# Keeping the state of a chunked scan for two heads' columns instead of four, and reading it in 32x64 tiles

## The chip, the cores and the metric

The kernel runs on one core of a Trainium2 chip. The metric is the device time of one execution in microseconds, as a median over several executions. Beside the timed runs, one execution was recorded by the hardware profiler. In its output PE is TensorE (matmuls), PEld its weight loads, DVE is VectorE, ACT is ScalarE, POOL is GpSimd and SP is SyncE, which here issues nearly all DMAs.

## What is computed

Two blocks follow each other. The first is a state-space scan in chunks (Mamba 2), for 4 batches, 8 heads, 768 positions, head dimension D = 32 and state dimension N = 16:

```python
for c in range(nc):                        # chunks of the sequence
    cum = np.cumsum(la, axis=-1)           # la = log a, inside the chunk
    L = np.exp(cum[:, :, :, None] - cum[:, :, None, :]) * causal
    M = einsum('bhin,bhjn->bhij', Cc, Bc) * L
    y_intra = einsum('bhij,bhjd->bhid', M, xc)
    y_inter = einsum('bhin,bhnd->bhid', Cc, state) * exp(cum)[..., None]
    y[:, :, sl] = y_intra + y_inter
    state = exp(sum(la)) * state + sum_j(B_j x_j * exp(cum_last - cum_j))
```

The second takes y as 3072 tokens of width 256: `h = x @ w_in` (to 2048), `g = h * sigmoid(1.702 h)`, `out = g @ w_out`. The weights arrive as float64, and the kernel turns them into float32 from their bits.

## The kernel before

The 3072 tokens are worked off in six groups of 512. A group is two *pairs* (PG = 2), a pair is two stretches of 128 positions, and each stretch has two halves of 64 positions. So the scan runs in chunks of 64, four to a pair (index `m` = 0 to 3, `k` = `m // 2` the stretch, `i` = `m % 2` the half). A batch has six stretches, that is three pairs; the state starts anew at pairs 0, 3, 6 and 9.

For a pair `p`, in this order:

- `load(p)` brings B, C and x by six DMAs on SP's queue, `spread(p)` brings the decays `a`, copied across the partitions, by two.
- `turn_only` transposes B and C on TensorE (L514) and copies the results out of PSUM into `BT`, `CT` (once for each of the two heads of a row group) and, for the first two pairs, a copy of C (L519 on ScalarE, L521 and L528 on VectorE). `since_start` multiplies C by the decay since the chunk's start: `CsT` (L546).
- `decay` makes the matrix L by a scan (L356), or `exps` by exponentials for pairs 0 and 1 (L497). `ends` weighs B by the decay to the chunk's end (L405).
- `gain` is the increment of the state, B times x, on TensorE (L591). Its result has a row per (head, n), 128 rows, and 64 columns: for each row group of 32 rows, that is two heads (Q = 2), the columns of both heads' x.
- `keep` (or `keep_both`) makes the states. `part_of` (L620) takes of each row only the columns of its own head, by a multiplication with a 0/1 matrix; `add_up` (L636) adds the decayed state of the chunk before.
- `score` is C times B (L560, 32x64 tiles); `weigh` (L571) multiplies it into L.
- `finish` makes y in two PSUM banks, one for each half `i`: `inter(0)` and `inter(1)` multiply the state with `CsT` (L663), and between them `intra` multiplies L with x (L684, 64x32 tiles). L708 copies y to SBUF as `yT`.

Before the change a state tile is 128 rows by HB * D = 128 columns: of a row (head, n) only the 32 columns of its head among four are not zero. `inter` uses one half of the rows at once (64 rows, four heads) with all 128 columns as the stationary operand. The two halves of the rows are two row tiles of TensorE, and they go to different banks: in `inter(0)` half `t = i`, in `inter(1)` the other. A tiny GpSimd memset (L694) between them keeps the two passes apart in each bank. The 0/1 matrix for `part_of` is `own`, 128 rows by four heads by 32, made once on GpSimd from `same` (L1019). `part` (L344) says for each row which of the two heads of its row group it belongs to.

The products of the second block use a scheme with seven products instead of eight on 2x2 blocks. `first(g, j, i)` is a step of the first product: digits are matmuls (L805 into a bank X, L815 into Y), D adds on VectorE (L930), S and T are the activation on ScalarE (L782). A string gives the order of the steps; "2.D" is step D of block j = 2. `mix_in`, `mix_y`, `mix_w`, `mix_g` make the sums that the scheme needs, on VectorE. The first group goes without this scheme (`hidden`, `half`, `project_all`: L729, L747, L847).

The order of instructions on each engine is the order in which the program emits them; `in_order` fixes it. So the place of a call in the program, or of a letter in a step string, decides what an instruction is queued behind. The weights are unpacked piece by piece by `fields`, `clamp`, `rounded` and `join` (L161, L164, L172, L173, L177, L188, L194), on VectorE and ScalarE, woven into the start and the first group. The second group (g = 1) begins with four `hidden` blocks in two steps "H0" and "H1"; after H1 the kernel before calls `gain`, `score`, `keep_both`, `weigh(n)`, `weigh(n + 1)` and `spread(3 * PG)`, with n = 4. Then comes the step string `2.1 3.1 2.5 ...`, whose `y` is `finish` for pairs 4 and 5 and whose `L` loads pair 7.

Of the kernel before, what the change touches and what calls it, by code (L numbers as in the profile page):

```python
# [8 lines left out]
FP32 = mybir.dt.float32  # L9
# [3 lines left out]
ALU = mybir.AluOpType  # L13
# [3 lines left out]
P = 128  # L17
# [18 lines left out]
def kernel(  # L36
# [31 lines left out]
    nc = tc.nc  # L68
# [5 lines left out]
    N = B.shape[-1]  # L74
# [136 lines left out]
    def spread(p):  # L211

        if p - 2 in ra:
            ra[p] = ra[p - 2]
        else:
            ra[p] = words(f"a{p}").bitcast(FP32)[:, :2 * NH * H].rearrange(
                "p (k e) -> p k e", k=2)
        b, c = divmod(2 * p, NC)
        for i, side in enumerate(SIDES):
            nc.sync.dma_start(  # L220
                out=ra[p][side],
                in_=scratch[b, c:c + 2, i].rearrange("c h i -> c (h i)").unsqueeze(
                    0).to_broadcast([H, 2, NH * H]))
# [91 lines left out]
    def pick_a(p):  # L315
# [19 lines left out]
    nc.gpsimd.affine_select(  # L335
        out=same, in_=same, pattern=[[N, NH], [0, D]], compare_op=ALU.is_ge,
        fill=0.0, base=N - 1, channel_multiplier=-1)

    own = const.tile([P, HB, D], FP32, name="own")
    idents = const.tile([P, 2 * NH, H], FP32, name="idents")  # L340


# [166 lines left out]
    def turn_only(p, engines=("ACT", "ACT", "ACT")):  # L509
        s = st[p] = {}  # L510
        tp = bank(f"tp{p}").rearrange("p (j k i) -> p j k i", j=2, k=2)
        for j, src in enumerate((rb[p], rc[p])):
            for k in range(2):
                nc.tensor.transpose(out=tp[:, j, k], in_=src[:, k].rearrange("p h n -> p (h n)"),  # L514
                                    identity=ident)

        def copy(engine, o, i, scale=1.0):
            if engine == "ACT":
                nc.scalar.activation(o, i, AF.Copy, scale=scale)  # L519
            else:  # L520
                nc.vector.tensor_single_scalar(out=o, in_=i, scalar=scale, op=ALU.mult)  # L521

        s["BT"] = ssd.tile([P, 2, P], FP32, tag="BT", name=f"BT{p}")
        copy(engines[0], s["BT"], tp[:, 0])

        s["CT"] = ssd.tile([P, 2, Q, P], FP32, tag="CT", name=f"CT{p}")
        if engines[1] == "DVE":
            nc.vector.tensor_tensor(  # L528
                out=s["CT"], in0=tp[:, 1].unsqueeze(2).to_broadcast([P, 2, Q, P]),
                in1=part.unsqueeze(1).unsqueeze(3).to_broadcast([P, 2, Q, P]), op=ALU.mult)  # L530
        else:
            for q in range(Q):
                copy(engines[1], s["CT"][:, :, q], tp[:, 1], part[:, q:q + 1])
        s["tp"] = tp[:, 1]
        if p < PG:

            s["tp"] = ssd.tile([P, 2, P], FP32, tag="CsT", name=f"C{p}", bufs=3)
            copy(engines[2], s["tp"], tp[:, 1])
# [27 lines left out]
    def weigh(p, ks=(slice(0, 2),)):  # L566

        Lv = Ls[p].rearrange("p k r q i -> p k r (q i)")
        cb = st[p]["cb"].rearrange("p r k e -> p k r e")
        for k in ks:  # L570
            nc.vector.tensor_tensor(out=Lv[:, k], in0=Lv[:, k], in1=cb[:, k], op=ALU.mult)  # L571
# [32 lines left out]
    def keep_both(pairs):  # L604

        for p in pairs:
            part_of(p, range(4))
        for p in pairs:
            add_up(p, range(4))

    def part_of(p, ms):
        if 0 in ms:
            state[p] = ssd.tile([P, 4, HB * D], FP32, tag="S", name=f"S{p}", bufs=3)
        new = state[p]
        ms = [m for m in ms if not last_chunk(p, m)]
        for i in range(2):
            ks = [m // 2 for m in ms if m % 2 == i]
            if ks:
                k, n = ks[0], len(ks)
                nc.vector.tensor_tensor(  # L620
                    out=new.rearrange("p (k s) (b e) -> p s k b e", s=2, b=HB // Q)[
                        :, i, k:k + n],
                    in0=increment[p][i][:, k:k + n].unsqueeze(2).to_broadcast(
                        [P, n, HB // Q, Q * D]),
                    in1=own.rearrange("p (b q) d -> p b (q d)", q=Q).unsqueeze(1).to_broadcast(
                        [P, n, HB // Q, Q * D]), op=ALU.mult)

    def add_up(p, ms):
        b, c = divmod(2 * p, NC)
# [10 lines left out]
    def finish(pairs):  # L640


        g, first = divmod(pairs[0], PG)
        y = [bank(f"y{pairs[0]}_{i}")[:, :NK * len(pairs) * 2 * H].rearrange(
            "p (t k i) -> p t k i", t=NK, i=H) for i in range(2)]
        begun, halves, seen = set(), {}, []

        def begin(i, parts):
            new = not begun & {(i, q) for q in parts}
            begun.update((i, q) for q in parts)  # L650
            return new

        def inter(flip):

            for n, p in enumerate(pairs):
                for k in range(2):
                    for i in range(2):
                        m, t = 2 * k + i, i ^ flip
                        if (4 * p + m) % (2 * NC) == 0:
                            continue  # L660
                        old = state[p][:, m - 1] if m else state[p - 1][:, 3]
                        rows = slice(HB * N * t, HB * N * (t + 1))
                        nc.tensor.matmul(  # L663
                            out=y[i][:, t, 2 * n + k], lhsT=old[rows],
                            rhs=st[p]["CsT"][rows, k, SIDES[i]],
                            start=begin(i, range(HB)), stop=False,
                            tile_position=(HB * N * t, 0), skip_group_check=True)
                        ins = tc.nc.cur_bb.bb.instructions[-1]
                        if not flip:
                            halves[i] = ins  # L670
                        elif seen:
                            tie(ins, seen.pop())

        def tie(ins, other):
            tc.add_manual_dep(ins, other.name, mybir.DependencyInfo(
                mybir.DependencyClass.Sync, mybir.DependencyReason.DATA), reason="same_bank")

        def intra(n, p):
            L = Ls[p]
            for k in range(2):  # L680
                for h in range(NH):
                    t, q = divmod(h, HB)
                    for i, side in enumerate(SIDES):
                        nc.tensor.matmul(  # L684
                            out=y[i][D * q:D * q + D, t, 2 * n + k], lhsT=rx[p][side, k, h],
                            rhs=L[side, k, h // Q, h % Q],
                            start=begin(i, (q,)), stop=True, tile_position=(H * i, D * q),
                            skip_group_check=True)

        if first == 0:  # L690
            yT[g] = ffn.tile([P, NK, TG], FP32, tag="yT", name=f"yT{g}")
        inter(0)

        nc.gpsimd.memset(spare, 0.0)  # L694
        seen.append(tc.nc.cur_bb.bb.instructions[-1])
        for other in halves.values():
            tie(seen[0], other)
        for n, p in enumerate(pairs):
            intra(n, p)
        inter(1)  # L700
        for p in pairs:
            state.pop(p - 1, None)
            st.pop(p)
            Ls.pop(p)
        cols = slice(2 * first * P, 2 * (first + len(pairs)) * P)
        to = early_y if pairs[0] == 0 else yT[g][:, :, cols]
        for i in range(2):
            nc.scalar.activation(  # L708
                to.rearrange("p t (k s i) -> p s t k i", s=2, i=H)[:, i], y[i], AF.Copy)
        if pairs[0] == 0:  # L710
            nc.gpsimd.tensor_copy(yT[g][:, :, cols], to)
# [291 lines left out]
    for r in range(2):  # L1003
# [4 lines left out]
    nc.vector.tensor_tensor(  # L1008
        out=idents, in0=ident[:, :H].unsqueeze(1).to_broadcast([P, 2 * NH, H]),
        in1=ident[:, H:].unsqueeze(1).to_broadcast([P, 2 * NH, H]), op=ALU.add)  # L1010
    turn_only(0, ("DVE", "DVE", "DVE"))
    since_exp()
    fields(0)
    clamp(0)
# [1 line left out]
    score((0,), ab0)  # L1016
    differ(1, [(r, ab[1, r]) for r in range(2)])
    exps(1, range(2))
    nc.gpsimd.tensor_tensor(out=own, in0=same[:, :HB], in1=same[:, HB:], op=ALU.add)  # L1019
    ends(0, 0, nc.gpsimd)  # L1020
    ends(0, 1, nc.gpsimd)
    weigh(0)
# [72 lines left out]
    for k, i in enumerate((9, 13)):  # L1095
# [5 lines left out]
    later = n, n + 1  # L1101
    at(after, "H0", lambda: decay(n), lambda: decay(n + 1), lambda: turn(n), lambda: turn(n + 1))
    at(after, "H1", lambda: gain(later), lambda: score(later),
       lambda: keep_both(later), lambda: weigh(n), lambda: weigh(n + 1), lambda: spread(3 * PG))
    assert [b for b in range(NB) if 3 * CG <= b * NC < 4 * CG] == [2]


# [51 lines left out]
            keep_both(pairs)  # L1159

    def more_loads():
        load(p + 1)
        spread(p + 1)

    run(1, "2.1 3.1 2.5 2.6 3.6 2.2 2.7 3.5 3.7 3.2 2.D 2.4 3.D 3.4 2.S W 2.3 3.S 3.3 2.T 3.T y L",
        y=lambda: finish(later), W=lambda: mix_w(0), L=more_loads)
    for j in range(2):
        mix_g(1, j)
    run(1, "4.1 P P 4.6 P P 4.7 P 4.5 P 4.2 P 4.D", seven(1, 0))
# [97 lines left out]
```

## Time and profile before

| | |
|---|---|
| median of 4 runs | 368.65 us (367.99 to 372.68) |
| profiled execution, whole | 368.83 us |
| its span | 367.0 us |
| TensorE busy | 359.5 us, 98% |
| VectorE busy | 250.7 us, 68% |
| ScalarE busy | 150.9 us, 41% |
| GpSimd busy | 12.1 us, 3% |
| granted TensorE clock | 1.0 |

Busy times are shares of the span. The profile counts a float32 matmul as two records, and as two weight loads. Durations of neighbouring matmuls overlap, so that a group's mean is longer than what one of its matmuls adds to the time. In the chain of waits each piece is followed back to what released it; there a stretch of matmuls has the time from its own start to the next one's.

### The profile page before, as it was taken

The numbers are of one execution on the slowest core, as the hardware profiler recorded it, in microseconds if no ns is written. First come the engines' busy times: TensorE is split into PE (matmuls) and PEld (weight loads), VectorE is DVE, ScalarE is ACT, GpSimd is POOL, SyncE is SP. The second block draws the span as 40 slices with busy tenths as digits, with TensorE's granted clock in tenths as the row PEclk, the third lists the DMA queues.
The fourth block names the chain that finished last, engine by engine and source line by source line (L and its number), as shares of the span: only waits on it lengthen the run. The fifth ranks groups of instructions, "written<-read, shape, count | busy, mean of one in ns | idle before, by whom it ended". The sixth has DMA issues, their size and how long they took to land.

```text
span 367.0 us, 8730 instructions
## 1 busy us (share of the span) xinstructions
PE 359.5 (98%) x3740; PEld 309.4 (84%) x3740; DVE 250.7 (68%) x473; ACT 150.9 (41%) x341; POOL 12.1 (3%) x42
## 2 busy tenths in 40 slices
PE   8999999999999999999999999999999999999996
PEld 4774468896779999879999989999988999989996
DVE  5989979997757998558577466576474355374353
ACT  5759563213432432544433444333435331453320
POOL 4300000000000000000000000000000000000000
PEclk9999999999999999999999999999999999999999
DMA  9998599056853300075200062000010000010001
GB/s 157 232 338 143 169 198 184 4 127 122 142 101 46 92 9 2 28 140 66 60 1 2 2 111 64 2 0 2 1 61 2 0 3 0 2 57 2 0 2 57
DMA packets 86045, 25.03 MB, mean 68 GB/s; under 512 B 76152, under 2 KB 79480, under 8 KB 86008
## 3 DMA queue, kind: packets, MB, share of 16 engines
q1 hardware_dynamic: 83416, 24.03, 30.2%
q10 hardware_dynamic: 2592, 0.46, 0.7%
q8 instruction: 29, 0.48, 0.5%
q14 instruction: 8, 0.07, 0.1%
HBM read 21.23 MB, written 3.24 MB: 67 GB/s over the span
## 4 chain that ended last, share of the span: by engine, by line
PE 83%; issue 7%; DVE 7%; ACT 1%; DMA 1%; ACTq 0%; POOL 0%; DVEq 0%
PE acc L911 31%; PE X L805 16%; PE Y L815 12%; PE o L847 8%; PE h L729 6%; PE y L663 3%; PE y L684 2%; PE cb L560 2%; PE tp L514 1%; PE A L591 1%; DVE p L188 1%; DVE m L177 1%; DMA az<-in_a_dram 1%; DVE w_in L194 1%; DVE p L161 1%
## 5 line engine op out<-in xcount | busy, mean ns | idle before, releaser
L911 PEld LDWEIGHTS acc<-mw,mg 128*128 128x128 f32 x480 | 67.5, 191 | 4.2
L911 PE MATMUL acc<-mw,mg 128*128 128x128 f32 x480 | 69.1, 275 | 0.0
L930 DVE TENSOR_TENSOR gT<-Y,ac 128x512 f32<-128x512 f32 x38 | 26.1, 690 | 54.3 <-PE Y L815 36.0
L810 ACT ACTIVATE ac<-X 128x256 f32<-128x256 f32 x76 | 29.1, 383 | 80.7 <-PE X L805 80.2
L782 ACT ACTIVATE gT<-gT 128x512 f32<-128x512 f32 (+1 forms) x76 | 39.4, 520 | 37.6 <-DVE gT L930 37.1
L911 PEld LDWEIGHTS acc<-w_out,gT 128*128 128x128 f32 x320 | 44.1, 191 | 2.5
L805 PE MATMUL X<-my,mi 128*128 128x256 f32 x152 | 45.7, 383 | 0.1
L911 PE MATMUL acc<-w_out,gT 128*128 128x128 f32 x320 | 45.2, 275 | 0.0
L930 DVE TENSOR_TENSOR gT<-Y,b 128x256 f32<-128x256 f32 x38 | 15.9, 420 | 28.9 <-PE Y L815 28.9
L729 PE MATMUL h<-yT,w_in 128*128 128x512 f32 x64 | 28.5, 595 | 0.2 <-DVE w_in L194 0.2
L847 PE MATMUL o<-w_out,gT 128*128 128x256 f32 x128 | 28.5, 381 | 0.0
L773 DVE TENSOR_TENSOR mg<-gT 128x512 f32<-128x512 f32 x40 | 27.3, 681 | 0.0
L847 PEld LDWEIGHTS o<-w_out,gT 128*128 128x128 f32 x128 | 23.9, 190 | 3.5 <-DVE w_out L194 0.2
L805 PEld LDWEIGHTS X<-my,mi 128*128 128x128 f32 x152 | 24.2, 191 | 1.7 <-ACT ac L810 0.5
L911 PEld LDWEIGHTS acc<-mw,gT 128*128 128x128 f32 x160 | 23.1, 191 | 1.8
L911 PE MATMUL acc<-mw,gT 128*128 128x128 f32 x160 | 24.3, 276 | 0.0
L911 PEld LDWEIGHTS acc<-w_out,mg 128*128 128x128 f32 x160 | 23.1, 191 | 1.4
L911 PE MATMUL acc<-w_out,mg 128*128 128x128 f32 x160 | 24.0, 275 | 0.0
L729 PEld LDWEIGHTS h<-yT,w_in 128*128 128x128 f32 x64 | 11.8, 190 | 14.1 <-issue 12.2
L815 PE MATMUL Y<-yT,mi 128*128 128x256 f32 x76 | 22.8, 383 | 0.3 <-DVE gT L930 0.3
L805 PE MATMUL X<-yT,w_in 128*128 128x256 f32 x76 | 22.9, 385 | 0.1
L815 PE MATMUL Y<-my,mi 128*128 128x256 f32 x76 | 22.8, 381 | 0.1
(139 smaller groups left out, 525.4 us busy)
## 6 DMA issues: line engine op xcount, KB each, us to landing
a<-scratch SPq DMA_DIRECT2D x18, 256.0 KB
bits<-in_moe_w_out_dram SPq DMA_DIRECT2D x4, 1024.0 KB
x<-in_x_dram SPq DMA_DIRECT2D x24, 128.0 KB
out_dram<-c SPq DMA_DIRECT2D x9, 256.0 KB
bits<-in_moe_w_in_dram SPq DMA_DIRECT2D x4, 512.0 KB
bits<-in_moe_w_in_dram SPq DMA_DIRECT2D x2, 1024.0 KB
b<-in_B_dram SPq DMA_DIRECT2D x24, 64.0 KB
c<-in_C_dram SPq DMA_DIRECT2D x22, 64.0 KB
```

The lines of the kernel that those rows point to most:

```text
L560: nc.tensor.matmul(out=s["cb"][side, r, k].rearrange("p (q i) -> p q i", q=Q), lhsT=BT[rows, k, side], rhs=CT[rows, k, :, side], start=Tru ...
L663: nc.tensor.matmul(out=y[i][:, t, 2 * n + k], lhsT=old[rows], rhs=st[p]["CsT"][rows, k, SIDES[i]], start=begin(i, range(HB)), stop=False, ...
L684: nc.tensor.matmul(out=y[i][D * q:D * q + D, t, 2 * n + k], lhsT=rx[p][side, k, h], rhs=L[side, k, h // Q, h % Q], start=begin(i, (q,)), s ...
L729: nc.tensor.matmul(out=h, lhsT=w_in[:, k, f * P:(f + 1) * P], rhs=yT[g][:, k], start=(k == 0), stop=(k == NK - 1))
L773: nc.vector.tensor_tensor(out=t[:, 0:2], in0=B[:, :, 1], in1=B[:, 0], op=ALU.subtract)
L782: nc.scalar.activation(o, i, AF.Silu, scale=GELU_SCALE)
L805: nc.tensor.matmul(out=s["X"], lhsT=lhsT, rhs=rhs, start=i == "1", stop=i == "4", skip_group_check=True)
L810: nc.scalar.activation(copy, s["X"], AF.Copy)
L815: nc.tensor.matmul(out=o, lhsT=lhsT, rhs=rhs, start=s.pop("new", False), stop=i != "5", skip_group_check=True)
L847: nc.tensor.matmul(out=o[k // 2][:, k % 2], lhsT=gT[g, f // 2][:, f % 2, k * P:(k + 1) * P], rhs=w_out[:, f], start=(f == 0 and k % 2 == 0 ...
L911: nc.tensor.matmul(out=o[k] if type(o) is list else o[:, cols], lhsT=h[:, cols], rhs=w, start=(j == 0 and (i, k) in begins), stop=(j == NF ...
L930: nc.vector.tensor_tensor(out=o, in0=v, in1=w, op=ALU.add)
```

## The change

The state tile gets Q * D = 64 columns instead of 128: each row keeps the columns of the two heads of its row group, of which those of its own head are not zero. `part_of` takes the increment's 64 columns once instead of twice, and multiplies them with `part`, spread over D, instead of `own`; `own` and the GpSimd operation that made it are gone. `inter` goes over row groups of 32 rows: one matmul of 64 rows by 128 columns becomes two of 32 rows by 64 columns, at the tile positions (32 r, 64 (r % 2)); r = 0 and 1 (or 2 and 3) write the lower and the upper 64 partitions of the same bank.

Three edits change the order. In `turn_only(0)` the third copy (of C) is on ScalarE instead of VectorE. In the second group, `weigh(n + 1)` is emitted after step 2.D (letter `w` in the string) instead of before the string. And `spread(3 * PG)` is emitted ahead of `load(p + 1)` in `more_loads`, after `finish`, instead of at the end of H1.

```diff
-    own = const.tile([P, HB, D], FP32, name="own")
...
-            state[p] = ssd.tile([P, 4, HB * D], FP32, tag="S", name=f"S{p}", bufs=3)
+            state[p] = ssd.tile([P, 4, Q * D], FP32, tag="S", name=f"S{p}", bufs=3)
...
                 nc.vector.tensor_tensor(
-                    out=new.rearrange("p (k s) (b e) -> p s k b e", s=2, b=HB // Q)[
-                        :, i, k:k + n],
-                    in0=increment[p][i][:, k:k + n].unsqueeze(2).to_broadcast(
-                        [P, n, HB // Q, Q * D]),
-                    in1=own.rearrange("p (b q) d -> p b (q d)", q=Q).unsqueeze(1).to_broadcast(
-                        [P, n, HB // Q, Q * D]), op=ALU.mult)
+                    out=new.rearrange("p (k s) (q d) -> p s k q d", s=2, q=Q)[:, i, k:k + n],
+                    in0=increment[p][i][:, k:k + n].rearrange("p k (q d) -> p k q d", q=Q),
+                    in1=part.unsqueeze(1).unsqueeze(3).to_broadcast([P, n, Q, D]),
+                    op=ALU.mult)
...
-                        rows = slice(HB * N * t, HB * N * (t + 1))
-                        nc.tensor.matmul(
-                            out=y[i][:, t, 2 * n + k], lhsT=old[rows],
-                            rhs=st[p]["CsT"][rows, k, SIDES[i]],
-                            start=begin(i, range(HB)), stop=False,
-                            tile_position=(HB * N * t, 0), skip_group_check=True)
...
+                        for r in range(2 * t, 2 * t + 2):
+                            rows, to = slice(32 * r, 32 * r + 32), Q * D * (r % 2)
+                            nc.tensor.matmul(
+                                out=y[i][to:to + Q * D, t, 2 * n + k], lhsT=old[rows],
+                                rhs=st[p]["CsT"][rows, k, SIDES[i]],
+                                start=begin(i, range(Q * (r % 2), Q * (r % 2) + Q)), stop=False,
+                                tile_position=(32 * r, to), skip_group_check=True)
...
-    turn_only(0, ("DVE", "DVE", "DVE"))
+    turn_only(0, ("DVE", "DVE", "ACT"))
...
-    nc.gpsimd.tensor_tensor(out=own, in0=same[:, :HB], in1=same[:, HB:], op=ALU.add)
...
-       lambda: keep_both(later), lambda: weigh(n), lambda: weigh(n + 1), lambda: spread(3 * PG))
+       lambda: keep_both(later), lambda: weigh(n))
...
     def more_loads():
+        spread(p)
         load(p + 1)
         spread(p + 1)
...
-    run(1, "2.1 3.1 2.5 2.6 3.6 2.2 2.7 3.5 3.7 3.2 2.D 2.4 3.D 3.4 2.S W 2.3 3.S 3.3 2.T 3.T y L",
-        y=lambda: finish(later), W=lambda: mix_w(0), L=more_loads)
+    run(1, "2.1 3.1 2.5 2.6 3.6 2.2 2.7 3.5 3.7 3.2 2.D w 2.4 3.D 3.4 2.S W 2.3 3.S 3.3 2.T 3.T y L",
+        w=lambda: weigh(n + 1), y=lambda: finish(later), W=lambda: mix_w(0), L=more_loads)
```

More of the change, by code (lines that the diff above doesn't have):

```diff
@@ L661, in inter @@
                         old = state[p][:, m - 1] if m else state[p - 1][:, 3]
-                        rows = slice(HB * N * t, HB * N * (t + 1))
-                        nc.tensor.matmul(
-                            out=y[i][:, t, 2 * n + k], lhsT=old[rows],
-                            rhs=st[p]["CsT"][rows, k, SIDES[i]],
-                            start=begin(i, range(HB)), stop=False,
-                            tile_position=(HB * N * t, 0), skip_group_check=True)
[L668 to L672, printed above, removed]
+                        for r in range(2 * t, 2 * t + 2):
[5 more added lines that the diff above has]
+                                tile_position=(32 * r, to), skip_group_check=True)
+                            ins = tc.nc.cur_bb.bb.instructions[-1]
+                            if not flip:
+                                halves[r] = ins
+                            elif seen:
+                                tie(ins, seen.pop())
         def tie(ins, other):
```

## The prediction

> **What bounds the kernel now.** I read the page first: share by engine, then the chain of waits, then the groups by form, and last the timeline of TensorE and VectorE around the places that the diff touches.
>
> ```profile
> span 367.0 us, 8730 instructions
> PE 359.5 (98%) x3740; PEld 309.4 (84%) x3740; DVE 250.7 (68%) x473; ACT 150.9 (41%) x341; POOL 12.1 (3%) x42
> PE acc L911 31%; PE X L805 16%; PE Y L815 12%; PE o L847 8%; PE h L729 6%; PE y L663 3%; PE y L684 2%; PE cb L560 2%; PE tp L514 1%; PE A L591 1%; DVE p L188 1%; DVE m L177 1%; DMA az<-in_a_dram 1%; DVE w_in L194 1%; DVE p L161 1%
> ```
>
> TensorE (PE) is busy 98% of the span and holds 83% of the chain. The edited matmuls, L663, have 3% of the chain, 11 us. So the state's VectorE work counts only where VectorE leads, and what L663 costs on TensorE counts nearly everywhere. The chain of waits shows where VectorE leads (start, length, what):
>
> ```profile
> 15.74 0.69 DVE w_in L194
> 17.14 0.98 DVE m L177
> 18.36 0.50 DVE S L636
> 19.49 0.70 DVE w_in L194
> 20.24 1.99 PE h L747 x8
> 34.36 1.24 DVE w_in L194
> 35.73 3.67 PE h L729 x8
> ```
>
> Up to about 36 us the chain goes mostly over VectorE, unpacking the weights; the state's operations stand in that queue. From 35.73 on it is TensorE with small gaps. The groups by form (count, busy us, mean ns, idle before) give the durations:
>
> ```profile
> L663 PE MATMUL y<-CsT,S 64*128 64x64 f32 x176 | 13.9, 279 | 0.8 <-issue 0.8
> L684 PE MATMUL y<-L,x 64*32 64x64 f32 x768 | 9.4, 225 | 0.6 <-issue 0.6
> L560 PE MATMUL cb<-CT,BT 32*64 32x128 f32 x352 | 6.7, 278 | 0.0
> L620 DVE TENSOR_TENSOR S<-A,own 128x256 f32<-128x256 f32 x18 | 6.6, 414 | 1.7 <-PE A L591 1.7
> L620 DVE TENSOR_TENSOR S<-A,own 128x128 f32<-128x128 f32 x8 | 2.2, 280 | 0.0
> L636 DVE SCALAR_TENSOR_TENSOR S<-S,since 128x128 f32<-128x128 f32 x32 | 11.1, 351 | 1.1
> ```
>
> The 88 matmuls of L663 show as 176 records, two per float32 matmul. They overlap, so 279 ns isn't their price; their spacing is. The timeline of weight loads (start, length, count) gives it:
>
> ```profile
> 93.98 0.96 PEld L560 LDWEIGHTS cb<-CT,BT 32*64 32x64 f32 x64
> 102.10 0.97 PEld L663 LDWEIGHTS y<-CsT,S 64*128 64x128 f32 x16 [0.33 <-ACT gT L782]
> 103.14 0.96 PEld L684 LDWEIGHTS y<-L,x 64*32 64x32 f32 x92
> ```
>
> Less one load's own length (187, 130, 105 ns by form), L663 goes at (0.97-0.19)/15 = 52 ns, L560 at (0.96-0.13)/63 = 13 ns, L684 at (0.96-0.11)/91 = 9.4 ns (10.2 where all its records are there). The few wide tiles are four to five times slower per record than the many small ones.
>
> **What the skill says.** The Trainium skill, "TensorEngine Tiling (Array Packing)", Key Properties: different tiles execute weight loads and matmuls in parallel, and a change of tiling mode drains the engine. The rates above agree with the first. The mode changes stay as many as before (64x128 or 32x64, then 64x32, then back), so their part of a stretch stays.
>
> "TensorE: Matmul & The Clock Gate", LDWEIGHTS: a load takes time by its columns, not its rows. The trace agrees: 128 columns 187 ns, 64 columns 130, 32 columns 105, that is 0.83 ns a column. So a record's load takes about 107 ns for 128 columns and 53 for 64. A matmul record streams at 0.84 ns a column (512 columns of L729 in 0.43 us), 53 ns for 64 and 107 for 128. One rule gives the measured rates: the larger of load and stream, divided by the tiles in use. L663: 107/2 = 53 (measured 52). L560: 107/8 = 13.4 (measured 13). L684: 53/8 = 6.7, measured about 10, which I take as an issue floor.
>
> "PSUM — Partial Sum Buffer", PSUM bank collisions: different column tiles may write one bank at once in disjoint partitions, two row tiles into one bank and quadrant may not. The new tiles r = 0 and 1 share bank 0, but in partitions 0-63 and 64-127; r = 2 and 3 likewise in bank 1. So nothing has to be serialised; no run yet shows such a pair.
>
> "Runtime: NRT & Kernel Launch", Instruction fetch mechanics: instructions arrive in blocks of 256, mostly hidden. The page of before has 29 packets (0.48 MB) on the instruction queue q8, and the trace doesn't agree that all is hidden; see the second rival.
>
> **The change part by part.**
>
> 1. *Inter matmuls.* Each 64x128 record becomes two 32x64 records. By the rule a record costs max(53, 53)/4 = 13.3 ns. One pass of a group is now 16 records (14 where a batch starts) and takes 1.04 to 1.09 us from its start to the next stage, mean 1.06: 15 x 52 ns plus some 0.23 us of first load and drain. After: 31 x 13.3 + 0.23 = 0.64 us. Bounds: 10 ns each (the floor) gives 0.55; 27 ns, if load and stream of a tile don't overlap ((53+53)/4), gives 1.07. I take 0.64, since the rule fits L663 and L560 at once, and no overlap would make L663 80 ns. Five groups of two passes stand on the TensorE path: 10 x (1.06-0.64) = 4.2 us, with ends 0 and 5.1. The pairs 0 and 1 are handled in the start.
>
> 2. *State on VectorE.* An L620 over two chunks goes from 256 to 128 elements, 414 to 280 ns: -0.13. Over one chunk, 280 less 66 = 214. An L636 goes from 351 to 285 (the slope is 132 ns per 128 elements). After the start this hides behind TensorE except in part 4. The broadcast `part` operand is like L528, which runs at the ordinary rate; if it were slow, the gain here would be nothing.
>
> 3. *Start.* The third copy of `turn_only(0)`, 415 ns, leaves VectorE for ScalarE (395 ns by the L519 row). ScalarE stands idle 0.40 us there until 9.44, waiting for `rows`, so the copy fits; without this cover `since_exp` would be late by 0.4. VectorE gains 0.33, but `ends(1)` at 14.62 then waits for the exponentials of ScalarE (they end at 14.49), which come only some 0.1 earlier: 0.1 is kept. `keep(1, (0,))` gives 0.14 more, so `half(1,0)` starts at about 20.0 instead of 20.24. `finish((1,))` has two passes of 8 records, 0.59 and 0.64, which become 15 x 13.3 + 0.2 = 0.4: -0.4. Its result goes over L708, `clamp(2)` on ScalarE (VectorE waits 1.26 us for that at 26.29) and the weights to 35.73. Together -0.65, with ends 0 and -1.0. The removed `own` (454 ns on GpSimd at 5.35) frees nothing: GpSimd then waits 3.31 us for ScalarE.
>
> 4. *`weigh(5)` behind 2.D.* Now both L571 stand ahead of 2.D and 3.D:
>
> ```profile
> 97.87 2.35 DVE L571 TENSOR_TENSOR L<-L,cb 128x1024 f32<-128x1024 f32 x2
> 100.14 1.28 DVE L930 TENSOR_TENSOR gT<-Y,ac 128x512 f32<-128x512 f32 x2
> 100.87 1.30 PE L815 MATMUL Y<-yT,mi 128*128 128x256 f32 x4 [0.31 <-DVE gT L930]
> ```
>
> TensorE is ready for 2.3 at 100.56, gets it at 100.87, and 3.3 only after 3.D at 101.42: some 0.74 lost. After: `keep_both` is 4 x 0.13 + 8 x 0.066 = 1.05 shorter, so the first L571 starts at 96.8 and ends at 98.0. 2.D waits for the copy that ends at 98.83 and ends at 99.5, in time for 2.3. Queued behind it, `weigh(5)` ends at 100.7 and 3.D at 101.3; 3.3 wants it at 101.0. Left: 0.3, so -0.4 (ends 0 and -0.75). The intra matmuls of pair 5 come after 102 and wait for nothing.
>
> 5. *`spread(6)` later.* On SP's queue it still stands between `spread_rows(2)` and `load(7)`, for no other DMA lies in between in the program. It issues two DMAs as before, ahead of `load(7)`'s six and `spread(7)`'s two: 0.
>
> 6. *Instruction supply.* 176 more matmul records and as many loads, in the densest stretches. Two stretches already stall for "issue":
>
> ```profile
> 105.21 0.27 PE L684 MATMUL y<-L,x 64*32 64x64 f32 x2 [0.61 <-issue]
> 162.60 0.32 PE L663 MATMUL y<-CsT,S 64*128 64x64 f32 x2 [0.83 <-issue]
> ```
>
> If the stall ends at a fixed moment, what was gained ahead of it in the same stretch is lost: 0.42 in the first, up to 0.84 in the second, 1.26 together. Bounds 0 and 1.26 here; I take 0.6.
>
> Sum: 4.2 + 0.65 + 0.4 - 0.6 = 4.65. The profiled execution took 368.83 (span 367.0, 1.8 around it): 368.8 - 4.65 = 364.2. The median of before, 368.65, is 0.2 lower, inside the spread of the runs. The measurement tells about 1% from no change, which is 3.7 us or 364.96.
>
> **The rivals.**
>
> *No gain in the passes.* The two records of one tile follow each other, so a load may not hide behind a stream of its own length (53 behind 53; L560 has 53 behind 107). Then 27 ns a record, 1.07 us a pass. For it: no row shows that balance. Against it: L663, with loads longer than streams, runs at the larger one, not at the sum. Only the 0.25 of VectorE's start and the 0.4 of part 4 stay: 368.2.
>
> *Slower by instruction supply.* Place: the five stretches of passes and intra. The stretch of pairs 4 and 5 has 2 x (16+128+16) = 320 instructions in 4.28 us, its stall included: 75 per us. If that is the supply, 384 take 5.1 us in each, 25.6, where the five take 3.49, 4.28, 4.42, 3.55 and 3.59 = 19.3 now. That is +6.3, less 1.05 from parts 3 and 4: 374.1. It decides below 384 x 5/(19.3+1.05) = 94 per us. For it: the two stalls. Against it: three of five stretches have none, and the intra runs at 256 in 1.41 us, 180 per us.
>
> *More gain.* The passes run at the floor, 0.55, and no stall eats anything: 368.8 - 5.1 - 0.65 - 0.4 = 362.7.
>
> **How the numbers follow.** The forecast, 364.2 with its own range 363.0 to 366.0, gets 0.58; no gain 0.24; slower 0.10; more gain 0.08. The range, 362.8 to 368.4, takes in the no-gain case and leaves out the slower one and the lower tail. Faster by over 1%: four fifths of the forecast (0.47) and more gain (0.08), 0.55. Within 1%: the rest of the forecast and no gain, 0.35. Slower: 0.10.
>
> **What would show it.** Right: L663 has 352 records, passes of 0.6 to 0.7 us in the chain, weight loads 13 ns apart; L620 280 and 214 ns, L636 285; `half(1,0)` at 20.0; the h matmuls of 35.73 at about 35.1; 2.3 without a wait for VectorE, 3.3 with 0.3. Wrong: passes still about 1 us, or "issue" stalls of over a microsecond in the five stretches.

## The result and the profile after

| | before | after |
|---|---|---|
| median | 368.61 us (64 runs, 367.24 to 372.87) | 367.27 us (43 runs, 364.98 to 371.02) |
| ratio, 95% interval | | 0.9955 [0.9936, 0.9973] |
| profiled execution, its span | 368.83, 367.0 us | 366.25, 364.2 us |

The change gains 1.3 us in the median and 2.6 us in the profiled execution, where 4.6 were forecast. The two differ because some executions show a granted TensorE clock below 1.0 and are mostly 1 to 5 us longer: 24 of 44 of after (0.988 to 0.997), and 21 of the 97 executions of before that stood beside the experiments (0.982 to 0.991, and two far lower, at 412 and 537 us). The profiled execution of after is not one of them. The ratios, here and below, leave out executions over 1.5% above the fastest of their kernel, so they aren't the quotients of the medians.

The page of after: span, busy times, and q8, the queue that brings instructions.

```profile
span 364.2 us, 9080 instructions
PE 354.5 (97%) x3916; PEld 304.5 (84%) x3916; DVE 245.4 (67%) x472; ACT 150.8 (41%) x342; POOL 11.1 (3%) x41
...
q8 instruction: 31, 0.51, 0.6%
```

TensorE has 176 matmul records more and is busy 5 us less. q8 has two packets more. The groups by form (count, busy us, mean ns, idle before) of the edited lines; L660, L618 and L632 are L663, L620 and L636 of before:

```profile
L660 PE MATMUL y<-CsT,S 32*64 32x64 f32 x352 | 9.1, 225 | 1.6 <-issue 1.6
L632 DVE SCALAR_TENSOR_TENSOR S<-S,since 128x64 f32<-128x64 f32 x32 | 8.9, 284 | 1.1
L618 DVE TENSOR_TENSOR S<-A,part 128x128 f32<-128x128 f32 x18 | 4.2, 281 | 1.7 <-PE A L589 1.7
L618 DVE TENSOR_TENSOR S<-A,part 128x64 f32<-128x64 f32 x8 | 1.6, 214 | 0.0
```

The VectorE durations are the forecast ones. L660 has 352 records, but stands idle 1.6 us for "issue", twice as long as L663. The chain of waits (start, length, what) shows both:

```profile
211.70 0.67 PE y L660 x24
212.37 1.41 PE y L681 x89
213.78 0.62 PE y L660 x28
214.40 0.41 PE X L802
214.81 0.88 issue
215.69 0.92 PE X L802 x3
...
268.13 0.67 PE y L660 x30
268.80 1.41 PE y L681 x91
270.22 0.38 PE y L660 x15
270.60 1.60 issue
272.20 0.50 PE y L660 x17
```

A pass takes 0.62 to 0.67 us, as forecast. Shortly behind one pass, and inside another, TensorE stops for 0.88 and 1.60 us. In before, the stops were in pairs 4 and 5 (0.61) and 6 and 7 (0.83); now they are in pairs 8 and 9 and in 10 and 11. The start and part 4, in the timeline (in brackets: idle time and what ended it):

```profile
16.73 0.58 DVE L161 TENSOR_SCALAR p<-bits 128x512 uint32<-128x512 uint32 x1 [0.57 <-DMA bits<-in_moe_w_in_dram]
20.00 0.69 DVE L194 SCALAR_TENSOR_TENSOR w_in<-m,p 128x512 f32<-128x512 f32 x1
21.37 1.99 PE L744 MATMUL h<-y,w_in 128*128 128x256 f32 x8 [1.72 <-DVE S L632]
36.48 3.67 PE L726 MATMUL h<-yT,w_in 128*128 128x512 f32 x8 [0.21 <-DVE w_in L194]
101.27 0.70 PE L812 MATMUL Y<-yT,mi 128*128 128x256 f32 x2 [0.34 <-DVE gT L927]
```

`half(1,0)`, L744, starts at 21.37 instead of the forecast 20.0, and hidden(0,8), L726, at 36.48 instead of 35.1 (before: 35.73). Its weights, L194, end at 20.69, so 0.68 us of its wait has another cause than VectorE.

**Where the stops lie.** Number TensorE's weight loads, matmuls and semaphore instructions in the order of the trace, with the drain that opens the program as number 0. The instruction behind each stop is then 2497 and 3777 in before, and 705, 5313 and 6593 in after. All five are 193 more than a multiple of 256. q8's packets are 16 KiB; the Trainium skill, "Runtime: NRT & Kernel Launch", Instruction fetch mechanics, gives that size as a block of 256 instructions, so the stops lie at block limits. In after, the packet of the block at 5313 starts 1.0 us after TensorE has come within 299 instructions of it, takes 1.2 us, and its first instruction runs another 1.2 us later: 3.35 us in all. For 6593 it is 3.73, for 3777 of before 3.89; for 2497 of before, whose packet starts 3.05 us after that point, it is 5.67. The 299 is an estimate from the packets: with 295, a packet would start before its point is reached. The skill calls this fetch mostly hidden. In these stretches it isn't: passes and intra are now 384 instructions in 2.65 us, so that 299 of them are used up before the next block is there.

### The profile page after: what moved, and what is told of

The parts are those of the page before. It is cut to its first block, busy times and chain, and to the rows that moved or that the text cites. A ratio compares the mean times of both kernels' runs of the same rounds, so it can differ in the third digit from the quotient of the medians.

```text
span 364.2 us, 9080 instructions
## 1 busy us (share of the span) xinstructions
PE 354.5 (97%) x3916; PEld 304.5 (84%) x3916; DVE 245.4 (67%) x472; ACT 150.8 (41%) x342; POOL 11.1 (3%) x41
## 4 chain that ended last, share of the span: by engine, by line
PE 88%; DVE 5%; SPq 2%; DMA 2%; issue 1%; ACT 1%
PE acc L908 34%; PE X L802 18%; PE Y L812 13%; PE o L844 8%; PE h L726 6%; PE y L681 2%; SPq L123 2%; PE y L660 2%; PE cb L558 2%; DMA bits<-in_moe_w_in_dram 1%; PE tp L512 1%; PE A L589 1%; DVE p L188 1%; DVE m L177 1%; DMA az<-in_a_dram 1%
## 5 line engine op out<-in xcount | busy, mean ns | idle before, releaser
L726 PE MATMUL h<-yT,w_in 128*128 128x512 f32 x64 | 28.5, 595 | 0.2 <-DVE w_in L194 0.2
L726 PEld LDWEIGHTS h<-yT,w_in 128*128 128x128 f32 x64 | 11.8, 190 | 14.1 <-issue 12.2
```

The lines of the kernel that those rows point to most:

```text
L726: nc.tensor.matmul(out=h, lhsT=w_in[:, k, f * P:(f + 1) * P], rhs=yT[g][:, k], start=(k == 0), stop=(k == NK - 1))
```

## The experiments

Theory: what the passes gain is there, and is eaten by stops at block limits that happen to fall into a dense stretch, in the start too. Rivals: the order edits eat it, or the small tiles do. The main tool is an added piece of work that nobody uses: the products go to `h` and are cleared by the h matmuls that follow. One such matmul is four instructions, and 48 take 0.95 us.

```diff
         h = bank(f"h{g}_{f}")
+        if (g, f) == (0, 8):
+            for m in range(48):
+                r = slice(32 * (m % 4), 32 * (m % 4) + 32)
+                nc.tensor.matmul(out=h[r, :32], lhsT=ones[r, :32], rhs=ones[r, :32], start=True,
+                                 stop=True, tile_position=(32 * (m % 4), 32 * (m % 4)),
+                                 skip_group_check=True)
```

All results; "rest" is the time in the profiled execution from the first h matmul of hidden(0,8) to the end of the span, so without the start and, but for the last row, without the added matmuls (329.65 and 334.7 hold lost clock too). The ratio is to the executions of before that stood beside each kernel.

| kernel | median us | ratio, 95% | rest us |
|---|---|---|---|
| before | 368.61 | | 331.27 |
| after | 367.27 | 0.9955 [0.9936, 0.9973] | 327.72 |
| state and passes alone | 368.14 | 0.9966 [0.994, 0.9993] | 329.65 |
| order edits alone | 368.93 | 0.9993 [0.996, 1.0027] | 329.8 |
| after, 48 added | 373.03 | 1.0067 [1.0038, 1.0096] | 334.7 |
| after, 192 added | 364.15 | 0.9844 [0.9801, 0.9888] | 324.92 |
| before, 144 added | 368.41 | 0.999 [0.9958, 1.0022] | 329.64 |
| after, 256 added in one place | 373.94 | 1.0103 [1.0053, 1.0152] | |
| after, 256 added in four places | 370.48 | 1.0011 [0.9986, 1.0036] | |
| state alone, 192 added | 364.74 | 0.9902 [0.9869, 0.9936] | 324.96 |
| after, 200 added, both start edits | 363.75 | 0.9859 [0.9828, 0.989] | 324.93 |
| after, 192 added, weight piece earlier | 363.94 | 0.9867 [0.9809, 0.9925] | 324.96 |
| after, 200 added, no filling | 363.69 | 0.9834 [0.979, 0.9877] | 324.89 |
| after, 192 added at 189 us | 364.88 | 0.9863 [0.9813, 0.9914] | 326.06 |

### 1. State and passes alone

The kernel after with the order of before:

```diff
-    turn_only(0, ("DVE", "DVE", "ACT"))
+    turn_only(0, ("DVE", "DVE", "DVE"))
...
-       lambda: keep_both(later), lambda: weigh(n))
+       lambda: keep_both(later), lambda: weigh(n), lambda: weigh(n + 1), lambda: spread(3 * PG))
...
-        spread(p)
...
-    run(1, "... 2.D w 2.4 ...", w=lambda: weigh(n + 1), ...)
+    run(1, "... 2.D 2.4 ...", ...)
```

> The kernel before with the 64-column state and the 32x64 passes alone; the order of before (third copy of C on VectorE, weigh(5) ahead of 2.D, spread(6) at the end of H1). TensorE's instructions are those of the changed kernel, in the same order. Theory (instruction supply: TensorE stalls where its instruction number reaches the end of a block of 256 inside a dense stretch): the stalls are where they are in the changed kernel, in the passes of pairs 8/9 and 10/11, 0.9 and 1.6 us in one profile, and the time is that of the changed kernel within 0.5 us, 366.5 to 367.8. Rival (the three order edits ate the gain): clearly faster than the changed kernel, about 364.2, as forecast for the passes.

Measured: 368.14 us, 0.3 above the expected band. The stops are those of after, at instructions 705, 5313 and 6593. So the order edits don't eat the gain. Its profiled execution is also one with less clock. The last stop in the timeline, and around it the view of windows (PE, PEld, DVE, ACT and POOL busy with counts, granted clock, DMA share, GB/s):

```profile
276.14 0.50 PE L660 MATMUL y<-CsT,S 32*64 32x64 f32 x18 [1.63 <-issue]
...
274.00:276.00 2.00, 0.52 (x27) 0.32 (x15) 0.00 (x0) 0.00 (x0) 0.00 (x0) 1.00 0.00 0
276.00:278.00 2.00, 1.84 (x22) 1.28 (x22) 0.00 (x0) 1.36 (x3) 0.00 (x0) 0.81 0.04 8
278.00:280.00 2.00, 2.00 (x10) 1.91 (x9) 0.69 (x1) 0.39 (x2) 0.00 (x0) 0.50 0.00 0
280.00:282.00 2.00, 2.00 (x14) 1.83 (x13) 0.00 (x0) 1.03 (x3) 0.00 (x0) 0.83 0.00 0
282.00:284.00 2.00, 2.00 (x16) 1.90 (x15) 1.24 (x3) 0.65 (x2) 0.00 (x0) 1.00 0.00 0
```

After a stop that leaves TensorE idle for 1.63 us the clock is half for about 3.4 us: the shares missing from 1.0 sum to 0.19 + 0.5 + 0.17 = 0.86 of 2 us, 1.7 us of work lost. The Trainium skill, "TensorE: Matmul & The Clock Gate", The HAM clock gate, has half clock after an idle window of about 3.4 us, and full clock after a busy one of that length. The trace agrees on half clock and on 3.4 us, but not on the idleness: here 1.63 us were enough. They aren't always: the other late stop of this execution, 1.67 us at instruction 5313, was followed by full clock.

### 2. Order edits alone

The kernel before with the three order edits, that is, the lines of experiment 1 the other way round.

> The kernel before with the three order edits alone; the state and the 64x128 passes of before. TensorE's instructions are those of before. Theory (instruction supply): stalls as before, in the stretches of pairs 4/5 and 6/7, and the time of before within 0.5 us (368.1 to 369.1). Rival (the order edits cost what the passes gain): about 3 us slower than before, 371.

Measured: 368.93, no difference from before that can be told. The two stops at 2497 and 3777 stay, with 0.21 and 0.30 us, and 3.3 waits 0.48 us for VectorE.

### 3 and 4. Other positions of the block limits

The piece above with `range(12)`, 48 instructions, and with `range(48)`, 192.

> The changed kernel with 12 float32 matmuls of 32x32 more ahead of the first matmul of hidden(0, 8), where TensorE waits 0.7 us for VectorE anyway; they write columns of the bank that the next matmul overwrites. They take 24 records and as many loads, 48 instructions, at about 10 ns a record 0.25 us, and move all later instructions by 48 against the blocks of 256. Theory (instruction supply), by a model with a block asked for 43 instructions before its predecessor is begun, 1.15 us to the DMA's start, at least 4.1 us from one to the next, and 2.45 us to use: four stalls of 1.6 to 1.8 us in the stretches of pairs 4/5, 6/7, 8/9 and 10/11, 6.9 us against 2.8 in the changed kernel: 4 us slower than it, 371. Rival (the stalls come from semaphores or from PSUM, not from the number of an instruction): 0 to 0.3 us slower than the changed kernel, stalls where they were.

> The same with 48 matmuls, 192 instructions, some 1 us of TensorE of which 0.7 are idle anyway. Theory (instruction supply), by the same model: no stall in any of the five stretches, so 2.5 us less than the changed kernel, less some 0.3 us for the added matmuls: 364.5 to 365, 1% faster than before. Rival: 0.3 to 1 us slower than the changed kernel, since it has four times the added work of the kernel with 48.

Measured: 373.03 and 364.15 us, 2 us above and 0.35 below what was expected. The chain of waits of the first, and then the passes in the chain of the second:

```profile
105.85 1.43 issue
161.29 1.54 issue
220.09 1.43 issue
278.45 1.54 issue
```

```profile
74.52 0.62 PE y L660 x28
76.56 0.62 PE y L660 x28
102.49 0.62 PE y L660 x32
104.52 0.62 PE y L660 x32
156.79 0.61 PE y L660 x26
158.81 0.61 PE y L660 x28
212.24 0.67 PE y L660 x24
214.32 0.62 PE y L660 x28
267.79 0.67 PE y L660 x30
269.87 0.64 PE y L660 x32
```

With 48 added there are four stops, at 2753, 4033, 5313 and 6593, and only 3 of 22 executions keep the full clock; in the profiled one it is 0.982. With 192 there is none of these stops, and "rest" is 9.8 us shorter: 5.9 of that is the idle time of the four stops, and 3.4 is clock, since two of them were each followed by 3.4 us at half clock. The ten passes sum to 6.30 us. This kernel beats before and after.

### 5. Before without stops

The piece with `range(36)`, 144 instructions, in the kernel before.

> The kernel before, with 36 matmuls of 32 rows by 32 columns (144 instructions of TensorE, their products are cleared by what follows) ahead of the h matmuls of hidden(0,8). Theory of the instruction blocks: all later block limits move by 144 instructions, out of the dense stretches, so the two issue stalls of before (0.61 and 0.83 us) go and none comes. That is 1.4 us less, and some 0.3 for the added matmuls: a span near 365.9, about 1 us under the median of before. The difference between this kernel and the kernel after with 192 added instructions (364.15) is then what the state and the passes are worth when no stall is in the way: 3 to 4 us. Rival, the added work itself helps TensorE: then this kernel also comes to about 364. Rival, the stalls have nothing to do with the count of instructions: they stay near 105 and 162 us, and the time is that of before plus 0.3.

Measured: 368.41 us, a span of 366.3 with hidden(0,8) 0.9 us later; the stops are gone. "Rest" falls by 1.63 to 329.64, where 1.4 was expected. The later hidden(0,8), mostly the added matmuls, takes more than half of that back: before, beside it, took 368.81, and no gain can be told. The added work doesn't itself help, then, and the time of 364 needs the new passes. Against 324.92 they, the state and the order edits are worth 4.7 us where neither kernel stops. Two of its passes in the chain:

```profile
103.12 1.04 PE y L663 x16
271.00 1.09 PE y L663 x16
```

All ten are two of 1.04 us in each of the first two stretches, two of 1.03, then 1.09 and 1.04, and two of 1.09: 10.53, that is 4.23 more than above.

### 6 and 11. The control: one whole block more

`range(64)`, 256 instructions; then the same in four places:

```diff
-        if (g, f) == (0, 8):
-            for m in range(64):
+        if (g, f) in ((0, 8), (0, 9), (0, 10), (0, 11)):
+            for m in range(16):
```

> The kernel after, with 64 such matmuls (256 instructions, one whole block) in hidden(0,8). Theory of the instruction blocks: the limits fall on the same instructions of the program as in the kernel after, so the two issue stalls of 1.5 to 1.8 us come back in the same stretches (pairs 8 and 9, pairs 10 and 11), and the time is that of after plus 0.3 to 0.8: 367 to 368.5. Rival, any added work of this kind takes the stalls away: about 364.5.

> The control again, with its own fault removed: 256 added instructions as in the kernel that took 373.94, but 64 in each of hidden(0,8) to hidden(0,11), so that they make no dense stretch of their own. Theory of the instruction blocks: the limits fall on the same instructions of the program as in the kernel after, the two issue stalls come back in pairs 8 and 9 and in pairs 10 and 11, and the time is that of after plus what the added matmuls take, 1.2 us: executions at full clock 366.5 to 367.5, a median of 367.5 to 369. Rival, the added work in the first group is what helps: 364 to 365, and no such stalls.

Measured: 373.94 and 370.48 us. In both the stops come back at the same instructions of the program, 5569 and 6849. In time both missed their expectation. In the first, the added piece was itself a dense stretch and stopped at a block limit inside (at 1217), where the packet had only started at 39.93:

```profile
42.28 0.31 PE L728 MATMUL h<-ones 32*32 32x32 f32 x12 [2.05 <-issue]
...
222.07 0.38 PE L808 MATMUL X<-my,mi 128*128 128x256 f32 x1 [1.19 <-issue]
```

The second has no such stop. Its profiled execution, at full clock, has a span of 366.1 us, 1.9 above after's; the added matmuls are 1.5 of that (four times 0.38). Its median is 1.5 us above the expected band, since 18 of its 22 executions lost clock (the four others have a median of 368.05); why so many more than of after, isn't known. Added work that doesn't move the limits in the program doesn't help.

### 7. The order edits without stops

Experiment 1 with 192 added.

> The state and the passes of the kernel after with the order of the kernel before (weigh(5) and spread(6) in H1, three copies of turn_only(0) on VectorE), and 192 added instructions in hidden(0,8) as in the kernel that took 364.15. No issue stalls are expected in either. What is left is the worth of the order edits without stalls. Reading of the traces: 2.3 and 3.3 wait for VectorE in neither, as keep_both is 1 us shorter, so the later weigh(5) is worth 0 to 0.2 us: 364.0 to 364.4. Rival, the step of the forecast (the later weigh(5) is worth 0.4): 364.5. Rival, the earlier weigh(5) is the better place now: 363.6.

Measured: 364.74 us, outside the expected band, but with six executions not to be told from 364.15. "Rest" is 324.96 against 324.92: nothing, as the first reading had it. But it is a sum of two. Here neither 2.3 nor 3.3 waits for VectorE:

```profile
101.80 1.03 PE L818 MATMUL Y<-yT,mi 128*128 128x256 f32 x4
102.76 0.69 PE L660 MATMUL y<-CsT,S 32*64 32x64 f32 x32
```

From the increments (L589) to the passes it takes 8.38 us, the kernel with 192 added and the later `weigh(5)` 8.80, before without stops 8.93. The 0.3 comes back at 125.6, where here, and in before, X waits some 0.33 us for ScalarE, which waits for VectorE behind the scan L426:

```profile
125.56 0.30 PEld L808 LDWEIGHTS X<-my,mi 128*128 128x128 f32 x2 [0.34 <-ACT ac L813]
```

With the order of after this wait is gone. Which of the edits takes it away wasn't tried.

### 8, 9 and 10. The start

The DMAs of weight piece 1 ahead of `load(1)`, and `half(1,0)` without its two filling matmuls (eight instructions): both, the first, the second.

```diff
     fetch(0)
+    fetch(1)
     load(1)
-    for i in range(1, 4):
+    for i in range(2, 4):
         fetch(i)
...
-    half(1, 0, 2)
+    half(1, 0)
```

> The kernel after with 200 added instructions in hidden(0,8), the DMAs of weight piece 1 issued ahead of load(1), and half(1,0) without the two filling matmuls. Theory of the start: VectorE's lead of 0.3 us from the shorter state work is lost because it runs into the landing of weight piece 1 (wait at L161, 0.57 us in the kernel after), and because the limit of an instruction block falls at the 705th instruction, the first of the second run of h matmuls. With the piece earlier and the eight instructions gone, L161 of piece 1 starts without a wait for its DMA, the second run of h matmuls starts at about 20.3 instead of 21.2 to 21.4, and the time is 0.7 to 1 us under the kernel with 192 added instructions: 363.2 to 363.5. Rival, what follows in the start waits for something else (load(1) lands later and holds VectorE): no gain, 364 or more.

> The kernel after with 192 added instructions in hidden(0,8) and, of the start's two edits, only one: the DMAs of weight piece 1 are issued ahead of load(1). Theory A (the landing of the piece is what ate VectorE's lead): L161 of piece 1 has no DMA wait, VectorE's w_in of piece 1 ends at about 20.4, but the limit of a block still falls on the 705th instruction, so TensorE gets on at 21.2 or later: 0 to 0.3 us of gain against 364.15, that is 363.9 to 364.2. Theory B (the landing alone decides): all of the 0.4 to 1 us that the two edits gave together: 363.2 to 363.7.

> The kernel after with 200 added instructions in hidden(0,8) and the start's other edit alone: half(1,0) without its two filling matmuls, so that the 705th instruction lies in the middle of the second run of h matmuls, as in the kernel before. Weight piece 1 still lands late in some executions. If the block limit decides the start, this alone gives most of the gain (363.2 to 363.7); if the landing decides, nothing (364.0 to 364.4), and TensorE stands idle for up to 2.4 us ahead of half(1,0), which may cost granted clock.

Measured: 363.75 us (0.25 above its band), 363.94 and 363.69 us; from each other and from 364.15 this can't be told with six executions each. The profiles tell the two causes apart. With the piece earlier, L161 starts at 16.10 without a DMA wait and the weights end at 19.86, but L751, whose first instruction is again the 705th, starts 0.7 later. Without the filling it starts 0.15 us after the weights, which end at 20.78:

```profile
20.57 1.99 PE L751 MATMUL h<-y,w_in 128*128 128x256 f32 x8 [0.87 <-DVE S L633]
```

```profile
20.09 0.69 DVE L194 SCALAR_TENSOR_TENSOR w_in<-m,p 128x512 f32<-128x512 f32 x1
20.93 1.97 PE L750 MATMUL h<-y,w_in 128*128 128x256 f32 x8 [1.10 <-DVE S L618]
```

With both, the shortest spans of all kernels are seen, 360.7 us in two of six executions; its profiled one waited 1.56 us for ScalarE at 12.74, lost clock, and shows nothing of the start.

### 12. The added work late

The kernel after with the 48 matmuls at the head of `turn_only(8)`, near 189 us, instead of in hidden(0,8).

> The kernel after with the 192 added instructions not in the first group but ahead of the transposes of turn_only(8), near 189 us. Everything before is the kernel after: start, stretches of the first three groups. Theory of the instruction blocks: only the block limits after 189 us move, which takes the two stalls of pairs 8 to 11 away (2.8 us) for 1.0 us of added work. Executions at full clock: a span of 362.1 where after has 363.9; the median 364 to 364.7, lower than after by 2.5 to 3, as the losses of granted clock go with the stalls. Rival, what the padding in hidden(0,8) did was something in the first group: no gain, 367 to 368.5.

Measured: 364.88 us, 2.4 us under after and 0.2 above what was expected; at full clock a span of 362.2, where 362.1 was expected. Only the two late stops were taken away. Its start shows the stop at 705 alone: the weights end at 19.97, and TensorE starts 3.4 us later, when the packet that lands at 21.82 has come into use.

```profile
19.28 0.69 DVE L194 SCALAR_TENSOR_TENSOR w_in<-m,p 128x512 f32<-128x512 f32 x1
...
23.38 3.66 PE L751 MATMUL h<-y,w_in 128*128 128x256 f32 x8 [3.61 <-DVE S L625]
```

The name in the bracket is that of the last semaphore event, an operation long before; the instruction number names the cause.

## Why the prediction was wrong

Wrong in size, right in sign: 364.2 us was forecast, 367.27 came. That lies inside the range only because the range took in the case of no gain in the passes, which isn't what happened. Its steps, with the measured value:

| step | forecast us | measured us |
|---|---|---|
| 1 passes | -4.2 | -4.23 (10.53 to 6.30) |
| 2 VectorE durations | 280, 214, 285 ns | 281, 214, 284 ns |
| 3 start | -0.65 | +0.75 (35.73 to 36.48) |
| 4 `weigh(5)` | -0.4 | -0.13 in its place, -0.33 at 125 us |
| 5 `spread(6)` | 0 | no sign of it in the start or the rest |
| 6 instruction supply | +0.6 | +1.17 (1.63 to 2.80), and lost clock |
| sum | -4.65 | -2.77 (-2.8 in the span) |

The gain where nothing stops, 4.72 by "rest", is the passes and part 4: 4.23 + 0.13 + 0.33 = 4.69. Most of what is missing from 364.2 to 367.27 lies in three places: the start (1.4), the stops (0.6), and lost clock (1.3), which had no term.

- *Steps 1 and 2* were right. The rule "the larger of load and stream, over the tiles" gave the pass to 0.02 us, and the rival "no gain in the passes" falls. The tiles r = 0 and 1, which share a bank, didn't hold each other up: 32 records take 0.62 us.
- *Step 6 was mis-sized, and its mechanism was wrong.* It read the two stops of before as moments that stay in their stretches ("if the stall ends at a fixed moment, what was gained ahead of it in the same stretch is lost") and bounded the cost at 0 to 1.26. They are block limits. The change adds 351 instructions, which shifts every later limit against the program, and gives a dense stretch 64 more: the stops left the two stretches and came back in two others, with 2.80 us in place of 1.63, both worked out from "rest" against the kernels without stops.
- *Lost clock was put at nothing.* At full clock the median of after is 365.9 us; the other 1.3 up to 367.27 are clock. How much of it belongs to the stops isn't shown. In the profiled executions of all kernels half clock comes, ahead of the end, in 15 spells of 3.4 us, some directly behind one another: four follow a late stop, two follow the stop at 705, and nine lie between 13 and 24 us, with no such stop ahead of them. And the kernels without a late stop (experiments 4, 7 to 10 and 12) lost clock too, in 15 of 36 executions.
- *Step 3 has the largest error*: it failed by 1.4 us, outside its bounds of 0 and -1.0. VectorE had its lead, but ran into the landing of weight piece 1 (0.57 us at L161), and the 24 instructions that `finish((0,))` adds put the first h matmul of `half(1,0)` on a block limit, 705: 0.68 us. In before that limit was passed at 22.32 without a stop. The landing was not read for what a faster VectorE would meet. That part is in some measure chance: with the same start, L161 begins at 16.21 without a wait in the profile of experiment 12, and with the start of before it waits 0.41 us in that of experiment 5.
- *Step 4* saw the waits as they came (2.3 none, 3.3 0.34) and mistook their cause. Experiment 7 shows that the shorter `keep_both` alone takes both waits away (8.93 to 8.38); the later `weigh(5)` then puts 0.4 back. The later gain at 125 us, which makes up for it, wasn't foreseen.
- The rival *slower by instruction supply* had the right resource and the wrong law. A rate of 75 instructions per us would slow all five stretches; three of them run at 384 in 2.65 us, 145 per us, without a stop. What decides is where the limits fall: with 48 more instructions it would have been right (373.03 us), with 192 there is nothing of it.

What stays open: in which places the executions lose clock that were not profiled, what brings half clock in the start, and why a packet starts sometimes 1.0, sometimes over 4 us after the instructions ahead of it have run out that far.

## What to carry to other kernels

When a kernel's matmuls get smaller and more, number TensorE's instructions and look at where each 256th falls: an "issue" stop belongs to a position in the instruction stream, and any edit ahead of it, even one that adds eight instructions, moves it or brings it. Before you judge a change by 1%, shift the blocks by some added instructions in both kernels and compare where neither stops; here that turned a measured 1.3 us into 4.3 by the medians (368.41 and 364.15) and 4.7 by "rest". And read what a lead will run into, a landing or a limit, before you count it.

## What was not expected of the hardware

- Past 45 us, stops at block limits leave TensorE idle for 0.2 to 1.9 us. All lie at instruction 193 modulo 256, in every kernel that has them. Each of the 14 limits in the profiles whose 299 instructions ahead were used up within 2.9 us stopped TensorE, by 0.3 us or more; five that left 3.7 to 3.8 us cost 0.1 at most. Three stops don't fit: at 2497 in before and in experiments 2 and 10 the packet itself started 2.6 to 7.6 us late.
- In the start the packets come later: in after the one for 705 starts 4.07 us after TensorE is within 299 instructions of it, in the kernel with the late padding 6.0 us, while the DMA engines' busy share is 90% and more. That the traffic delays them isn't shown.
- A stop of some 1.5 us can cost as much again: half clock for about 3.4 us. Of the 11 late stops of 1.2 to 1.9 us in the profiles, four were followed by it, and none of the six shorter ones. Of the kernel with four stops 3 of 22 executions kept the full clock, of the kernel before, with two of under a microsecond, 76 of 97.
